# Attention and a mixture of experts on one core: two row groups a slot sooner, and a new list of slots for one batch's token selection

## The chip, the core and the metric

The kernel runs on one core of a Trainium2 chip. The core has a matrix engine (PE, with its weight loads shown apart as PEld), a vector engine (DVE), a scalar engine (ACT), a general engine (POOL) and a queue engine that starts transfers (SP). Each runs its own list of instructions in order; semaphores join them. The metric is the time of one execution in microseconds of the device, the median of several.

## The reference, cut to what matters

Attention with a causal mask, then a top-1 mixture of experts in which each of 8 experts keeps its 80 best tokens by gate weight.

```python
scores = scale * np.matmul(q, k.transpose(0, 1, 3, 2))      # batch 8, heads 12, seq 448, dim 64, float32
scores = np.where(mask, -1000000000.0, scores)
attn = np.exp(scores - np.max(scores, axis=-1, keepdims=True))
attn = attn / (np.sum(attn, axis=-1, keepdims=True) + 1e-09)
x = np.matmul(attn, v)                                      # then (batch * seq, heads * dim) = 3584 x 768
logits = x @ w_gate                                         # 8 experts
expert_idx = np.argmax(logits, axis=1)                      # gate_w: the softmax weight of that expert
for e in range(E):
    tok_idx = np.where(expert_idx == e)[0]
    if len(tok_idx) > capacity:                             # 80
        tok_idx = tok_idx[np.argpartition(-gate_w[tok_idx], capacity)[:capacity]]
    h = np.maximum(x[tok_idx] @ w1[e], 0.0)
    out[tok_idx] = gate_w[tok_idx, None] * (h @ w2[e])
```

## The kernel before, in words

**The work.** Two heads make a pair; there are 6 pairs to a batch and 48 in all (pair 0 to pair 47). Attention runs as a pipeline over pairs. While the loop stands at pair i, PE issues the score products of pair i + 1 (`sp`, at the end of the pair), turns the exponentials of pair i - 1 (`tp`, four groups of four 128x128 transposes) and multiplies those of pair i - 2 by the values (`xp`, 16 matmuls). For pair i itself DVE makes the shifted scores (L444, seven pieces of 192, 192, 320, 320, 448, 448 and 64 columns, with their row minima) and ACT the exponentials (L448, the same seven). ACT copies the first three groups of `tp` to SBUF (L487), DVE the fourth; ACT copies `xp` into the batch's output `xu` (L510).

**The order.** The kernel writes the order out by hand. The loop gives each pair 8 slots, and each engine gets its instructions in the order in which the slots name them:

```python
TSLOT = [0, 1, 2, 4]                      # slots of the four tp groups
COPIED = {1: (0, 1), 2: (2,), 5: (3,)}    # slot: tp groups that are copied
SHIFTED = [0, 0, 1, 2, 3, 4, 4]           # slots of the seven pieces on DVE
VSLOT, XSLOT = 5, 6                       # xp, and its copy
```

In a slot first comes what these tables name (`tp`, `xp`, DVE's pieces, copies of `tp`, one exponential, the copy of `xp`), and then what the dictionary `plan` holds for that slot. `plan` holds what is done once per batch, in slots counted from the batch's end, that is, during the pairs of the next batch and the one after. There are two kinds of it.

- Row groups (`row_group`; `ROWS0` and `ROWS1`). A batch's output stands head by head in `xu`. A row group turns three 128x128 blocks back to token rows (`rt`, L604), DVE multiplies them by the reciprocal sums into `xr` (L623), and SP stores `xr` to `xs` in HBM (L628). A batch has eight; the two numbers of each are the slot of the turn and the slot of DVE's part.
- The selection (`STEPS`, and `EARLY` for the seventh batch, whose next batch is the last): `gp` and `lp` make the gate logits; `r0t` and `r1t` turn one-hot rows and weights (`selt`, L737) and `r0c`, `r1c` copy them to `ex`; `rl`, `lt` and `cp` count against the table of the batches before (`cp`, L780); `places` and `places2` are two DVE instructions that read `cp` into `rm` (L800); `c3w` to `c0w` multiply (`rn`, L751) and `c3l` to `c0l` compare (`less`, L754) inside the batch; `gt`, `own`, `rank`, `rr`, `tn`, `tab`, `rp`, `row` make the new table.

A batch's selection reaches into the pairs of the second batch after it: slot 52 (`cp`) is slot 4 of the pair at which the next batch has just ended. The first batch has no table before it and so no `cp`. So pairs 18, 24, 30, 36 and 42 have both the row groups of one batch and the `cp` of the batch before; pair 6 has row groups alone, and pair 12 row groups and comparisons. Below, these seven are called row pairs.

**The buffers.** All of `tp`, `xp`, `rt`, `cp`, `rn`, `gp`, `lp`, `selt`, `rl`, `gt`, `tn` and `rp` come from one pool of four PSUM buffers (`ps_g`, tag `g`); the score products have four others. A new tile of this pool can be written only when one of the four tiles before it has been read for the last time, and the pool gives it the buffer of one of these at build time.

**After attention** a tail written out by hand (`TAIL`) finishes the last pair and the last batch's selection; a gather (L1209) fetches the first expert's 80 rows, and with it SP starts the remaining weight loads (L222). Then come the two layers of the eight experts.

Of the kernel before, what the change touches and what calls it, by code (L numbers as in the profile page):

```python
# [24 lines left out]
SHIFTED = [0, 0, 1, 2, 3, 4, 4]  # L25
VSLOT, XSLOT = 5, 6
NORMS = [0, 2, 4]
ROWS0 = [(3, 5), (4, 6), (9, 10), (19, 20)]
ROWS1 = [(27, 28), (35, 36), (36, 38), (40, 41)]
STEPS = {'gp': 20, 'gs': 22, 'lp': 24, 'lg': 25, 'logit': 26, 'shifted': 27, 'chosen': 32, 'sums': 33, 'one_hot': 33, 'columns': 33, 'weight': 35, 'weighted': 36, 'parts': 37, 'r0t': 41, 'r0c': 42, 'r1t': 42, 'r1c': 43, 'rl': 44, 'lt': 46, 'c3w': 49, 'c3l': 50, 'cp': 52, 'ro': 53, 'places': 54, 'c2w': 56, 'c2l': 57, 'places2': 57, 'c1w': 58, 'c1l': 59, 'c0w': 59, 'c0l': 60, 'earlier': 60, 'gt': 65, 'own': 67, 'rank': 67, 'rr': 68, 'tn': 73, 'tab': 74, 'rp': 76, 'row': 78}  # L30
EARLY = {'gp': 16, 'gs': 18, 'lp': 24, 'lg': 25, 'logit': 26, 'shifted': 26, 'chosen': 28, 'sums': 29, 'one_hot': 29, 'columns': 29, 'weight': 30, 'weighted': 30, 'parts': 30, 'r0t': 32, 'r0c': 33, 'r1t': 33, 'r1c': 34, 'rl': 34, 'lt': 35, 'c3w': 35, 'c3l': 36, 'c2w': 36, 'c2l': 38, 'cp': 40, 'ro': 40, 'places': 41, 'c1w': 41, 'c1l': 42, 'c0w': 42, 'c0l': 43, 'places2': 43, 'earlier': 43, 'gt': 44, 'own': 45, 'rank': 45, 'rr': 46, 'tn': 49, 'tab': 49, 'rp': 52, 'row': 53}
THIRD = [0, 0, 2, 2, 4, 6, 8]
THIRD_EARLY = [0, 2, 4, 6, 6, 8, 9]
SECOND = [5, 6, 7, 8, 9, 10, 11]
# [13 lines left out]
def attention_then_moe(  # L48
# [907 lines left out]
    def later_on(slot, stages, gap=1):  # L956
        for x, f in enumerate(stages):
            plan.setdefault(slot + x * gap, []).append(f)
        return slot + len(stages) * gap

    def batch_plan(bt):

        ends = (bt.b * NP + NP) * SLOTS
        for x, f in zip(NORMS, norms(bt, slice(0, NP))):
            later_on(ends + x, [f])
        for g, rows in enumerate((ROWS0, ROWS1)):
            for t in range(NT):
# [5 lines left out]
        if CAP:  # L973
            steps.update(select_groups(bt))
        for name, at in (EARLY if bt.b == B - 2 else STEPS).items():
            if name in steps:
# [467 lines left out]
```

## Time and profile before

| | |
|---|---|
| median of 3 runs | 472.04 us (470.94 to 473.41) |
| profiled execution, its own time | 474.3 us |
| its span, first to last instruction | 472.5 us |
| mean granted TensorE clock | 0.987 |
| busy share of the span: PE, PEld, DVE, ACT, POOL | 92%, 70%, 81%, 83%, 51% |

The profiled execution's time is 1.8 us more than its span; its time is 2.3 us over the median of the runs. The busy shares are means over three stages: attention to about 327 us, the tail to about 355 us, and the experts. In a timeline row the first number is the start in us from the span's start, the second the stretch that the row's instructions took, then engine, line, operation, tiles (out<-in), shape, count, and in brackets the idle time of the engine just before and what ended it.

### The profile page before, as it was taken

What the parts mean: (1) busy time and instruction counts of PE and PEld (TensorE: products, weight loads), DVE (VectorE), ACT (ScalarE), POOL (GpSimd) and SP (SyncE); (2) the same over time, 40 slices, a digit from 0 to 9 for tenths busy, and PEclk for the clock granted to TensorE, in tenths of its full rate; (3) what the DMA queues carried; (4) which work ended last, traced back from release to release, by engine and by line L of the source; (5) the groups of instructions that cost most, each with busy time, mean ns of one, the idle gap of its engine ahead of it and who ended that gap; (6) DMA issues with size and microseconds to landing.
All of it is one profiled execution on the core that took longest, in us unless ns stands there. A gap on an engine that the chain in (4) does not pass through costs nothing.

```text
span 472.5 us, 15193 instructions
## 1 busy us (share of the span) xinstructions
PE 434.1 (92%) x5539; PEld 329.2 (70%) x5539; DVE 381.9 (81%) x1313; ACT 393.1 (83%) x1058; POOL 242.5 (51%) x359
## 2 busy tenths in 40 slices
PE   7799999999899899989989998989789999999894
PEld 3566677667567667756766775656549999999894
DVE  6676788978868887886888788696668999999991
ACT  5889999989879888987988898786477999899881
POOL 7957727718455851845575184510354265533511
PEclk9799999999999999999999999999989999999999
DMA  8454848748466563745665374359729999999941
GB/s 258 134 197 156 260 159 296 237 128 287 155 200 219 203 209 102 265 169 179 219 210 201 108 256 173 102 199 389 312 69 300 386 384 385 385 406 409 399 156 43
DMA packets 46666, 109.90 MB, mean 233 GB/s; under 512 B 5842, under 2 KB 23250, under 8 KB 45952
## 3 DMA queue, kind: packets, MB, share of 16 engines
q1 hardware_dynamic: 45392, 105.20, 63.3%
q0 software_dynamic: 1056, 3.51, 2.3%
q8 instruction: 43, 0.70, 0.6%
q14 instruction: 31, 0.25, 0.2%
q10 hardware_dynamic: 144, 0.23, 0.2%
HBM read 85.35 MB, written 23.99 MB: 231 GB/s over the span
## 4 chain that ended last, share of the span: by engine, by line
PE 65%; ACT 16%; issue 6%; DMA 5%; DVE 4%; POOL 3%; POOLq 0%; ACTq 0%; DVEq 0%
PE xp L505 18%; PE sp L425 11%; ACT PT L487 10%; PE tp L482 9%; ACT prob L448 5%; DMA wraw<-w 4%; PE gp L558 3%; PE hp L1242 2%; PE hp L1251 2%; PE hp L1249 2%; PE op L1252 2%; PE hp L1252 2%; PE rt L604 2%; PE op L1251 2%; PE op L1249 2%
## 5 line engine op out<-in xcount | busy, mean ns | idle before, releaser
L448 ACT ACTIVATE prob<-ns,nb 128x192 f32<-128x192 f32 (+3 forms) x336 | 176.0, 531 | 16.6 <-DVE nb L444 15.8
L444 DVE CUSTOM_DVE_ANT_0 ns<-sp,mask 128x192 f32<-128x192 f32 (+3 forms) x336 | 135.1, 445 | 47.2 <-PE sp L425 43.9
L482 PE MATMUL tp<-ident,prob 128*128 128x128 f32 x768 | 112.2, 280 | 4.5 <-ACT PT L487 4.2
L505 PE MATMUL xp<-PT,vt 128*64 128x448 f32 (+3 forms) x768 | 94.8, 389 | 10.4 <-issue 6.9
L373 POOL TENSOR_TENSOR qk<-qk,qk 128x448 f16<-128x448 f32 x94 | 96.7, 1044 | 7.1 <-DVE qk L401 3.9
L1173 DVE SCALAR_TENSOR_TENSOR wl<-wraw,wh 128x768 f16<-128x768 f32 (+1 forms) x98 | 97.3, 1060 | 1.7 <-POOL wl L1364 1.6
L487 ACT COPY PT<-tp 128x512 f32<-128x512 f32 x144 | 81.7, 586 | 15.8 <-PE tp L482 14.8
L505 PEld LDWEIGHTS xp<-PT,vt 128*64 128x64 f32 x768 | 52.3, 137 | 59.2 <-issue 32.8
L482 PEld LDWEIGHTS tp<-ident,prob 128*128 128x128 f32 x768 | 85.9, 143 | 9.0 <-ACT PT L487 6.7
L1188 ACT ACTIVATE wh<-wraw 128x768 f16<-128x768 f32 (+1 forms) x98 | 84.8, 925 | 3.2 <-PE hp L1252 0.9
L425 PE MATMUL sp<-qk 64*128 64x448 f16 (+2 forms) x864 | 68.3, 297 | 3.6 <-POOL qk L373 2.8
L1252 PEld LDWEIGHTS <-wl 128*128 128x128 f16 x668 | 66.7, 100 | 2.8 <-issue 2.7
L1249 PEld LDWEIGHTS <-wh 128*128 128x128 f16 x668 | 67.1, 100 | 1.9 <-issue 1.9
L1251 PEld LDWEIGHTS <-wh 128*128 128x128 f16 x668 | 66.7, 100 | 0.4 <-issue 0.3
L448 ACT ACTIVATION_READ_ACCUMULATOR prob<-ns,nb 128x1 f32 x336 | 65.7, 195 | 0.0
L1330 POOL DMA_INDIRECT out<-yo,idx x8 | 35.6, 4456 | 53.6 <-ACT yo L1327 50.4
L425 PEld LDWEIGHTS <-qk 64*128 64x128 f16 x864 | 36.4, 94 | 18.6 <-issue 2.9
L487 DVE COPY PT<-tp 64x256 f32<-64x256 f32 x144 | 43.6, 328 | 4.1 <-PE tp L482 2.0
L1251 PE MATMUL op<-hl,wh 128*128 128x80 f16 x324 | 36.8, 202 | 1.3 <-issue 1.3
L1249 PE MATMUL hp<-xh,wh 128*128 128x80 f16 x320 | 36.4, 202 | 1.1 <-issue 1.1
L1249 PE MATMUL op<-hh,wh 128*128 128x80 f16 x324 | 36.8, 202 | 0.3 <-issue 0.3
L1251 PE MATMUL hp<-xl,wh 128*128 128x80 f16 x320 | 36.2, 202 | 1.0 <-DVE xl L1228 0.7
(179 smaller groups left out, 659.4 us busy)
## 6 DMA issues: line engine op xcount, KB each, us to landing
wraw<-w SPq DMA_DIRECT2D x48, 384.0 KB
wraw<-w SPq DMA_DIRECT2D x30, 512.0 KB
out<-mask SPq DMA_DIRECT2D x56, 192.0 KB
qk<-k_t SPq DMA_DIRECT2D x23, 448.0 KB
qk<-q_t SPq DMA_DIRECT2D x23, 448.0 KB
vt<-v_t SPq DMA_DIRECT2D x24, 384.0 KB
xs<-xr SPq DMA_DIRECT2D x42, 192.0 KB
wraw<-w SPq DMA_DIRECT2D x5, 1536.0 KB
```

What stands on the lines that cost most here:

```text
L373: sub = lambda e, o, a, b: e.tensor_tensor(out=o, in0=a, in1=b, op=ALU.subtract)
L425: nc.tensor.matmul(pr.sp[t, j], a[rows, p, queries(t)], c[rows, p, FROM[t]:FROM[t] + WIDTH[t]], start=(x == 0), stop=(x == 2))
L444: nc.vector.tensor_tensor_reduce(out=ns, in0=pr.sp[x], in1=m, scale=-1.0 / 8.0, scalar=HUGE, op0=ALU.add, op1=ALU.min, accum_out=nb)
L448: nc.scalar.activation(pr.P[:, OFF[x]:OFF[x] + w], got[0], AF.Exp, bias=got[1], scale=-1.0, accum_out=pr.sums[:, h:h + 1])
L482: nc.tensor.transpose(tp[:, i * P:(i + 1) * P], f, ident)
L487: way(part_of(pr.PT, rows, to, *todims), part_of(got[0], rows, at, *dims))
L505: nc.tensor.matmul(xp[rows, c * P:S], st["vt"][:, c, p * P + j * DH:p * P + (j + 1) * DH], pr.PT[:, j, n0:n0 + w], start=(c == 0), stop=(c ...
L1173: return nc.vector.scalar_tensor_tensor(out=l, in0=src, scalar=SW, in1=h, op0=ALU.mult, op1=ALU.subtract)
L1188: nc.scalar.activation(h, src, AF.Copy, scale=SW)
L1249: nc.tensor.matmul(o, wh[:, ws], ah[:, c, :], start=(x == 0 and i % per == 0), stop=False, skip_group_check=True)
L1251: nc.tensor.matmul(o, wh[:, ws], al[:, c, :], start=False, stop=False, skip_group_check=True)
L1252: nc.tensor.matmul(o, wl[:, ws], ah[:, c, :], start=False, stop=(x == n - 1), skip_group_check=True)
```

## The change

Two row groups of every batch move. The turn of the first goes from slot 3 to slot 2 after the batch's end and DVE's part from 5 to 3; the turn of the second from 4 to 3 and DVE's part from 6 to 4. In `STEPS`, `places2` goes from 57 to 54, beside `places`; `ro` goes from 53 to 52 and issues nothing here, since 80 slots fit one chunk. The seventh batch gets another list.

```diff
-ROWS0 = [(3, 5), (4, 6), (9, 10), (19, 20)]
+ROWS0 = [(2, 3), (3, 4), (9, 10), (19, 20)]
...
-EARLY = {'gp': 16, 'gs': 18, 'lp': 24, 'lg': 25, 'logit': 26, 'shifted': 26, 'chosen': 28, 'sums': 29, 'one_hot': 29, 'columns': 29, 'weight': 30, 'weighted': 30, 'parts': 30, 'r0t': 32, 'r0c': 33, 'r1t': 33, 'r1c': 34, 'rl': 34, 'lt': 35, 'c3w': 35, 'c3l': 36, 'c2w': 36, 'c2l': 38, 'cp': 40, 'ro': 40, 'places': 41, 'c1w': 41, 'c1l': 42, 'c0w': 42, 'c0l': 43, 'places2': 43, 'earlier': 43, 'gt': 44, 'own': 45, 'rank': 45, 'rr': 46, 'tn': 49, 'tab': 49, 'rp': 52, 'row': 53}
+EARLY = {'gp': 18, 'gs': 20, 'lp': 24, 'lg': 25, 'logit': 26, 'shifted': 26, 'chosen': 28, 'sums': 29, 'one_hot': 29, 'columns': 29, 'weight': 30, 'weighted': 30, 'parts': 30, 'r0t': 33, 'r0c': 34, 'r1t': 35, 'r1c': 36, 'rl': 36, 'lt': 38, 'c3w': 40, 'c3l': 41, 'c2w': 41, 'c2l': 42, 'c1w': 42, 'c1l': 43, 'cp': 43, 'ro': 43, 'c0w': 44, 'c0l': 45, 'earlier': 45, 'places': 46, 'places2': 46, 'gt': 46, 'own': 47, 'rank': 47, 'rr': 47, 'tn': 49, 'tab': 49, 'rp': 52, 'row': 53}
```

On PE in pair 18 (and in the same way in 24, 30, 36 and 42), with `tp` the transposes of the pair before, `rt` the row groups, `cp` the rank counts and `xp` the product with the values:

```order
 L751 MATMUL rn<-ex 128x512
 L482 MATMUL tp<-ident,prob_108 128x128 x4
-L604 MATMUL rt<-ident,xu 128x128 x3
+L604 MATMUL rt<-ident,xu 128x128 x6
 L482 MATMUL tp<-ident,prob_108 128x128 x4
 L780 LDWEIGHTS lt
@@ -1032,5 +1030,4 @@
 L780 LDWEIGHTS lt
 L780 MATMUL cp<-oh_699,lt 80x8
-L604 MATMUL rt<-ident,xu 128x128 x3
 L505 MATMUL xp<-PT_113,vt_109 64x448 x2
```

Both row groups now stand before the fourth transposes. The four tiles before `xp` were `rt`, `tp`, `cp`, `rt` and are now `rt`, `rt`, `tp`, `cp`. In the built program `xp` took the buffer of the fourth transposes and waited for DVE's copy of them; now it takes the buffer of the first row group and waits for DVE's first `xr`.

On DVE in the same pair, before (the two 448-column pieces, the 64-column piece, the copies of the fourth transposes into `PT`, the first `xr`, the first `rm`, the second `xr`, the next pair's first piece):

```order
L444 ISA ns,nb<-sp,mask 128x448
L444 ISA nb 128x1
L444 ISA ns,nb<-sp,mask 128x448
L444 ISA nb 128x1
L444 ISA ns,nb<-sp,mask_86 128x64
L444 ISA nb 128x1
L487 COPY PT_114<-tp 64x2x2x64
L487 COPY PT_114<-tp 64x2x64 x2
L623 TENSOR_TENSOR xr<-rt,sums 128x384
L800 SCALAR_TENSOR_TENSOR rm<-cp,pnum,slots_e 80x320
L623 TENSOR_TENSOR xr<-rt,sums 128x384
L444 ISA ns,nb<-sp,mask 128x192
```

and now:

```order
L444 ISA ns,nb<-sp,mask 128x448
L444 ISA nb 128x1
L623 TENSOR_TENSOR xr<-rt,sums 128x384
L444 ISA ns,nb<-sp,mask 128x448
L444 ISA nb 128x1
L444 ISA ns,nb<-sp,mask_86 128x64
L444 ISA nb 128x1
L623 TENSOR_TENSOR xr<-rt,sums 128x384
L487 COPY PT_114<-tp 64x2x2x64
L487 COPY PT_114<-tp 64x2x64 x2
L800 SCALAR_TENSOR_TENSOR rm<-cp,pnum,slots_e 80x320 x2
L444 ISA ns,nb<-sp,mask 128x192
```

The first `xr` moved ahead of the pair's last two pieces, the second ahead of the copies into `PT`, and the second `rm` came up from the next pair. On SP the store of the first `xr` now stands ahead of one part of a weight load (or of one block of zeros for the output) instead of behind it.

On PE in pair 46, the second to last, in the seventh batch's selection, behind the last of the `rl` products:

```order
 L767 LDWEIGHTS ex
 L767 MATMUL rl<-row_1_709,ex 128x80
-L604 MATMUL rt<-ident,xu 128x128 x3
-L751 LDWEIGHTS ex
-L751 MATMUL rn<-ex 128x512
-L482 MATMUL tp<-ident,prob_108 128x128 x4
-L604 MATMUL rt<-ident,xu 128x128 x3
-L751 LDWEIGHTS ex
-L751 MATMUL rn<-ex 128x384
 L505 MATMUL xp<-PT_113,vt_109 64x448 x2
```

The two row groups and the fourth transposes now stand further up in the pair, the second turn of `selt` (from `mv`) after the third transposes instead of the second. The two largest `rn` moved into pair 47, where `xp` now stands behind all four `rn` and `gt` behind `xp`. In pair 44 `gp` moved from behind the first transposes to behind the third.

## Rows read from the trace of the kernel before

**Rows 1.** Busy time of the engines in stretches of the span: PE, PEld, DVE, ACT and POOL busy us (with instruction counts), granted clock, DMA share, GB/s. The first stretch is one batch, the others are the tail and the experts.

```profile
123.50:164.80 41.30, 38.76 (x407) 27.39 (x403) 33.59 (x147) 35.32 (x110) 23.19 (x40) 1.00 0.58 192
...
327.20:355.20 28.00, 23.84 (x190) 14.54 (x188) 17.15 (x60) 16.86 (x35) 11.71 (x16) 0.94 0.57 215
355.20:472.50 117.30, 105.72 (x2294) 103.63 (x2294) 104.86 (x122) 96.61 (x148) 45.58 (x14) 0.99 0.87 327
```

**Rows 2.** What PE's matmuls waited for: total us, times, longest.

```profile
PE xp L505 <- issue: 6.9, 5, 1.4
PE tp L482 <- ACT PT L487: 4.2, 8, 0.7
```

**Rows 3.** Timeline of PE in pair 18, from the first row group to `xp`.

```profile
118.59 0.49 PE L604 MATMUL rt<-ident,xu 128*128 128x128 f32 x3
...
119.35 0.28 PE L780 MATMUL cp<-oh,lt 128*80 128x8 bf16 x4
119.75 0.55 PE L604 MATMUL rt<-ident,xu 128*128 128x128 f32 x3
121.67 1.95 PE L505 MATMUL xp<-PT,vt 128*64 128x448 f32 x16 [1.38 <-issue]
```

**Rows 4.** Timeline of DVE over the same time, up to the first piece of pair 19.

```profile
119.03 0.41 DVE L537 RECIPROCAL sums<-sums 128x42 f32<-128x42 f32 x1
119.36 0.56 DVE L444 CUSTOM_DVE_ANT_0 ns<-sp,mask 128x448 f32<-128x448 f32 x1
...
119.84 0.62 DVE L444 CUSTOM_DVE_ANT_0 ns<-sp,mask 128x448 f32<-128x448 f32 x1
...
120.39 0.22 DVE L444 CUSTOM_DVE_ANT_0 ns<-sp,mask 128x64 f32<-128x64 f32 x1
...
120.65 0.92 DVE L487 COPY PT<-tp 64x256 f32<-64x256 f32 x3
121.49 0.54 DVE L623 TENSOR_TENSOR xr<-rt,sums 128x384 f32<-128x384 f32 x1
121.96 0.53 DVE L800 SCALAR_TENSOR_TENSOR rm<-cp,pnum,slots_e 80x320 bf16<-80x320 f32 x1
122.42 0.54 DVE L623 TENSOR_TENSOR xr<-rt,sums 128x384 f32<-128x384 f32 x1
124.53 0.36 DVE L444 CUSTOM_DVE_ANT_0 ns<-sp,mask 128x192 f32<-128x192 f32 x1 [1.57 <-PE sp L425]
```

**Rows 5.** Timeline of ACT over the same time: the copy of the third transposes, the exponential of the second 448-column piece, the copy of `xp`, and the first exponential of pair 19.

```profile
119.11 0.58 ACT L487 COPY PT<-tp 128x512 f32<-128x512 f32 x1
...
121.33 0.67 ACT L448 ACTIVATE prob<-ns,nb 128x448 f32<-128x448 f32 x1
...
123.66 0.53 ACT L510 COPY xu<-xp 128x448 f32<-128x448 f32 x1 [1.24 <-PE xp L505]
124.93 0.46 ACT L448 ACTIVATE prob<-ns,nb 128x192 f32<-128x192 f32 x1 [0.74 <-DVE nb L444]
```

**Rows 6.** Timeline of pair 19, the pair after: DVE's second `rm` and third `xr`, ACT's copy of the third transposes, and PE's fourth transposes.

```profile
126.36 0.54 DVE L800 SCALAR_TENSOR_TENSOR rm<-cp,pnum,slots_e 80x320 bf16<-80x320 f32 x1
...
127.22 0.55 DVE L623 TENSOR_TENSOR xr<-rt,sums 128x384 f32<-128x384 f32 x1
...
127.37 0.59 ACT L487 COPY PT<-tp 128x512 f32<-128x512 f32 x1
...
128.01 0.66 PE L482 MATMUL tp<-ident,prob 128*128 128x128 f32 x4 [0.57 <-ACT PT L487]
```

**Rows 7.** Timeline of pair 6, the first row pair: DVE's first 448-column piece and PE's `xp`.

```profile
42.41 0.56 DVE L444 CUSTOM_DVE_ANT_0 ns<-sp,mask 128x448 f32<-128x448 f32 x1
...
44.39 1.95 PE L505 MATMUL xp<-PT,vt 128*64 128x448 f32 x16 [0.37 <-ACT PT L487]
```

**Rows 8.** Timeline of the seventh batch's selection: the fourth transposes of pair 44; the second `selt`, DVE's two largest comparisons, an `rn` and `xp` of pair 46; the scores, the fourth transposes and `xp` of pair 47; and the first transposes of the tail.

```profile
301.37 0.66 PE L482 MATMUL tp<-ident,prob 128*128 128x128 f32 x4 [0.37 <-ACT PT L487]
...
313.78 0.40 PE L737 MATMUL selt<-identb,mv 128*128 128x128 bf16 x4 [0.84 <-POOL mv L722]
...
317.14 0.73 DVE L754 SCALAR_TENSOR_TENSOR less<-rn,ggw,before 128x512 bf16<-128x512 f32 x1
...
317.26 0.32 PE L751 MATMUL rn<-ex 128*128 128x384 bf16 x1 [0.61 <-DVE xr L623]
317.93 1.95 PE L505 MATMUL xp<-PT,vt 128*64 128x448 f32 x16 [0.35 <-DVE less L754]
...
319.22 0.60 DVE L754 SCALAR_TENSOR_TENSOR less<-rn,ggw,before 128x384 bf16<-128x384 f32 x1
...
319.81 1.40 PE L425 MATMUL sp<-qk 64*128 64x192 f16 x18
...
324.47 0.65 PE L482 MATMUL tp<-ident,prob 128*128 128x128 f32 x4 [0.71 <-ACT PT L487]
...
325.29 1.95 PE L505 MATMUL xp<-PT,vt 128*64 128x448 f32 x16
327.17 0.66 PE L482 MATMUL tp<-ident,prob 128*128 128x128 f32 x4
```

**Rows 9.** Timeline at the end of the tail: the gather of the first expert's rows on POOL, and SP's remaining weight loads.

```profile
350.56 1.08 POOL L1209 DMA_INDIRECT xg<-xs,idx  x1 [4.68 <-DVE gws L934]
...
355.32 16.15 SPq L222 DMA_DIRECT2D wraw<-w  x15
```

More of the change, by code (lines that the diff above doesn't have):

```diff
@@ L27 @@
 NORMS = [0, 2, 4]
-ROWS0 = [(3, 5), (4, 6), (9, 10), (19, 20)]
+ROWS0 = [(2, 3), (3, 4), (9, 10), (19, 20)]
 ROWS1 = [(27, 28), (35, 36), (36, 38), (40, 41)]
-STEPS = {'gp': 20, 'gs': 22, 'lp': 24, 'lg': 25, 'logit': 26, 'shifted': 27, 'chosen': 32, 'sums': 33, 'one_hot': 33, 'columns': 33, 'weight': 35, 'weighted': 36, 'parts': 37, 'r0t': 41, 'r0c': 42, 'r1t': 42, 'r1c': 43, 'rl': 44, 'lt': 46, 'c3w': 49, 'c3l': 50, 'cp': 52, 'ro': 53, 'places': 54, 'c2w': 56, 'c2l': 57, 'places2': 57, 'c1w': 58, 'c1l': 59, 'c0w': 59, 'c0l': 60, 'earlier': 60, 'gt': 65, 'own': 67, 'rank': 67, 'rr': 68, 'tn': 73, 'tab': 74, 'rp': 76, 'row': 78}
-EARLY = {'gp': 16, 'gs': 18, 'lp': 24, 'lg': 25, 'logit': 26, 'shifted': 26, 'chosen': 28, 'sums': 29, 'one_hot': 29, 'columns': 29, 'weight': 30, 'weighted': 30, 'parts': 30, 'r0t': 32, 'r0c': 33, 'r1t': 33, 'r1c': 34, 'rl': 34, 'lt': 35, 'c3w': 35, 'c3l': 36, 'c2w': 36, 'c2l': 38, 'cp': 40, 'ro': 40, 'places': 41, 'c1w': 41, 'c1l': 42, 'c0w': 42, 'c0l': 43, 'places2': 43, 'earlier': 43, 'gt': 44, 'own': 45, 'rank': 45, 'rr': 46, 'tn': 49, 'tab': 49, 'rp': 52, 'row': 53}
+STEPS = {'gp': 20, 'gs': 22, 'lp': 24, 'lg': 25, 'logit': 26, 'shifted': 27, 'chosen': 32, 'sums': 33, 'one_hot': 33, 'columns': 33, 'weight': 35, 'weighted': 36, 'parts': 37, 'r0t': 41, 'r0c': 42, 'r1t': 42, 'r1c': 43, 'rl': 44, 'lt': 46, 'c3w': 49, 'c3l': 50, 'cp': 52, 'ro': 52, 'places': 54, 'c2w': 56, 'c2l': 57, 'places2': 54, 'c1w': 58, 'c1l': 59, 'c0w': 59, 'c0l': 60, 'earlier': 60, 'gt': 65, 'own': 67, 'rank': 67, 'rr': 68, 'tn': 73, 'tab': 74, 'rp': 76, 'row': 78}
+EARLY = {'gp': 18, 'gs': 20, 'lp': 24, 'lg': 25, 'logit': 26, 'shifted': 26, 'chosen': 28, 'sums': 29, 'one_hot': 29, 'columns': 29, 'weight': 30, 'weighted': 30, 'parts': 30, 'r0t': 33, 'r0c': 34, 'r1t': 35, 'r1c': 36, 'rl': 36, 'lt': 38, 'c3w': 40, 'c3l': 41, 'c2w': 41, 'c2l': 42, 'c1w': 42, 'c1l': 43, 'cp': 43, 'ro': 43, 'c0w': 44, 'c0l': 45, 'earlier': 45, 'places': 46, 'places2': 46, 'gt': 46, 'own': 47, 'rank': 47, 'rr': 47, 'tn': 49, 'tab': 49, 'rp': 52, 'row': 53}
 THIRD = [0, 0, 2, 2, 4, 6, 8]
```

## The prediction

> **What bounds the kernel now.** I read the stretches first. In a batch of attention PE is busy 38.76 of 41.30 us, ACT 35.32, DVE 33.59, POOL 23.19, and the transfers take 0.58 of the DMA engines [rows 1]. So PE paces attention, and what can be won there without less work is its idle 2.5 us per batch. Where that lies, PE's waits tell: `xp` waited 6.9 us, five times, 1.4 at the longest, with no engine named ("issue"), and `tp` 4.2 us, eight times, for ACT's copies [rows 2]. Five times 1.4 is 6.9: it is one wait that repeats, and the timeline puts it into pair 18, where `xp` starts at 121.67 after 1.38 us idle [rows 3]. The rows of DVE say why: its copy of the fourth transposes starts at 120.65 and the next instruction at 121.49; `xp` starts as soon as it has ended (120.65 + 0.92 = 121.57) and well before the first `xr` ends (122.03) [rows 4]. So `xp` waits for a buffer, that of the fourth transposes, which DVE empties only behind three pieces of the softmax. The data that `xp` multiplies are a pair old. In pair 19 the fourth transposes start at 128.01 after 0.57 idle; ACT's copy of the third ends at 127.37 + 0.59 = 127.96: again a buffer [rows 6].
>
> The end moves with attention's end. The first gather stands at 350.56 and the remaining weight loads start behind it at 355.32 [rows 9]; from there the transfers take 0.87 of the DMA engines, in the tail before only 0.57 [rows 1]. The loads have no head start that a shorter attention could use up, so I let every us won in attention count once in the end.
>
> **The row pairs with `cp` (18, 24, 30, 36, 42).** Nothing is added or removed: the same transposes, multiplications and stores stand elsewhere. `xp` now takes the buffer of the first row group. When is that free? DVE's first 448-column piece ends at 119.36 + 0.48 (starts 119.36 and 119.84), by then the reciprocals (119.03 + 0.41) and the turn (118.59 + 0.49) are done, so `xr` runs from 119.84 to 120.38 with the 0.54 of its own row [rows 3, 4]. The 0.07 from 121.57 to PE's start, taken over with the matmul's 0.03 behind its weights, gives `xp` at 120.48 instead of 121.67: 1.19 us. PE itself would be ready at about 120.0: `cp`, last before `xp` now, waits for ACT's copy of the third transposes (119.11 + 0.58 = 119.69), as the second row group does now at 119.75, and takes 0.28 [rows 3, 5]. So a wait of some 0.3 to 0.4 stays.
>
> What pays for it is the two `xr` ahead of softmax pieces. The second 448-column piece ends 0.47 later, at 120.39 + 0.47 = 120.86; ACT takes it up at 121.33 [rows 4, 5], so the delay is covered with 0.4 to spare. Were that cover gone, the exponentials and then the copies that free buffers would be late by what is missing. Behind it DVE runs without a gap: from 119.84 two `xr` (0.47 each from start to start), the pieces (0.55 and 0.26), the copies (0.84) and two `rm` (0.46 each) make 3.5 us, to 123.35 [rows 4]. The next pair's first piece starts at 124.53, on scores that come 1.19 sooner now, at 123.34 [rows 4]. So DVE is just in time. It loses its 1.57 us of idle, and ACT its 1.24 and some of its 0.74 [rows 5]. Each 0.1 by which I have DVE too fast costs 0.1 per batch.
>
> **The pair after (19, 25, 31, 37, 43).** The second `rm`, at 126.36, is gone from here, 0.46 of DVE's time, so the third `xr` ends at 127.22 + 0.55 - 0.46 = 127.31. The fourth transposes take its buffer and start at 127.37 instead of 128.01; `xp` behind them takes the third transposes' buffer, free at 127.96 as before, where it used to follow the fourth transposes (128.01 + 0.66, less some 0.07 that matmuls overlap) [rows 6]. It starts at about 128.04 instead of 128.6: 0.55 us.
>
> Both together are 1.74 us for each of five batches, 8.7 us. Bounds: 1.19 alone (ACT or DVE keep the second), 5.95; all idle of both rows, 5 x (1.38 + 0.57) = 9.75.
>
> **Pairs 6 and 12.** Pair 6 has no `cp`. There `xp` waits 0.37 for ACT's copy of the third transposes [rows 7]; now it takes the first row group's buffer, whose `xr` can end at 42.41 + 0.56 + 0.54 = 43.51, before PE is there. 0.3 us, between 0 and 0.37. In pair 12 the buffers of `xp` and of the transposes before it stay those of the same copies: nothing.
>
> **The seventh batch's list.** In pair 44 `gp` comes behind the third transposes, so the fourth no longer wait 0.37 for ACT's copy of these [rows 8]: 0.4 us with the pipeline's drain. In pair 46 PE waits 0.84 for POOL's `mv`, 0.61 for an `xr` and 0.35 for a comparison, and `xp` starts at 317.93 [rows 8]. Now the fill before `mv` is a group of transposes and a row group more, the two `rn` are gone, and `xp` waits for DVE's copy of the second `selt`: `mv` at 313.78 as now, two pieces, an `xr` and the copy behind it, about 316.1. So pair 46 is 1.8 us shorter. Pair 47 takes over the two `rn` and DVE's two comparisons (0.73 and 0.60), and `xp` there waits for the third comparison behind them: 5.85 us after the pair's scores by DVE's durations, where it is 325.29 - 319.81 = 5.48 now; `gt` follows `xp` and waits for the last comparison. The tail's first transposes come 8.3 us after the scores instead of 327.17 - 319.81 = 7.36 [rows 8]. So 0.9 of the 1.8 is given back. The list is worth 0.4 + 0.9 = 1.3 us; bounds are all its waits, 0.37 + 0.84 + 0.61 + 0.35 + 0.71 = 2.9, and, since the last pair's chain through DVE is long and I add it up by hand, a loss of 1.5 (its 0.9 more, and the 0.6 of one comparison that PE would stand behind in the tail).
>
> **The queues.** SP now stands at the first store until its `xr` is done, with one weight part or zero block behind it. Those parts are multiplied only after 355 [rows 9], so this is free. POOL's order does not change.
>
> **Sum.** 8.7 + 0.3 + 1.3 = 10.3 us. The profiled execution's 474.3 would be 464.0, its span 472.5 would be 462.2; the median of the runs, 2.3 lower than the profiled time, goes from 472.04 to 461.7.
>
> **The rivals.**
> *Half of it.* The bubble at `xp` shrinks, and the rest is eaten by DVE, which has no slack left, or by the last pairs. 5.95 alone gives 466.1. For it: DVE's 0.01 us of margin. Against: DVE has less to do in the pair after.
> *All of it.* PE never waits in these places: 9.75 + 0.37 + 2.9 gives 459.0. Against: the first `xr` ends at 120.38 by the rows, and PE is ready earlier.
> *The idle moves and nothing is won.* ACT is busy 35.32 of 41.30 us, 86%, PE's weight loads only 27.39, 66% [rows 1]; if ACT paces the batch, PE's bubble is only where the surplus shows, and each bubble closed opens another. Then only the seventh list counts: 470.7. Against: ACT itself idles 1.24 for `xp` behind the bubble and 0.74 more [rows 5], and 6 us per batch in all. The Trainium skill, Perfetto Trace Analysis, section Identifying the Most-Contended Engine, says this: matmul busy time is no measure of the tensor engine's headroom, weight-load busy time is, and for the other engines occupancy tells the one to work on. By that rule ACT is the engine here, and the time stays near 471. The trace's waits of ACT for PE speak against it in these pairs.
> *Slower.* DVE is late with the first `xr`: 1.2 us later than I have it and `xp` starts no sooner than now; if it came only behind DVE's copies, at 122.41 (121.57 + the 0.94 of two `xr` - 0.1 of gaps now there), each of the five batches would lose 0.74, 3.7 us, and with the list's loss of 1.5 the time would be 477.2, without it 475.7. It decides itself at whether `xr` ends before 121.57. Against: all that it needs is there by 119.84.
>
> **How the numbers follow.** The forecast (459.5 to 464.5) gets 0.62, half of it (464.5 to 468.5) 0.20, all of it 0.08, nothing won 0.06, slower 0.04. The range 458.5 to 467.5 takes in the bounds of the first three and leaves out some 0.15. Half a percent, about what a measurement of this kernel can tell from no change, is 2.4 us: faster 0.90, same 0.06, slower 0.04.
>
> **What would show it.** In the trace after: `xp` of pair 18 with 0.2 to 0.5 us idle instead of 1.38, released by the first `xr`; a batch of 39.5 us instead of 41.2; the fourth transposes of pair 19 with no wait for ACT; DVE without the 1.57 us before pair 19's first piece; pair 46 near 7.8 us and pair 47's first tail transposes about 8.3 us after its scores. The prediction is wrong if DVE's first piece of pair 19 comes late after its scores, if ACT's copies become what `tp` and `xp` wait for elsewhere in the batch, or if the tail or the experts grow by what attention loses.

## The result and the profile after

The changed kernel takes 460.12 us (median of 4 runs, 459.66 to 461.18); the kernel before took 471.58 beside it (470.94 to 473.41). The ratio is 0.9754, with a 95% interval from 0.9721 to 0.9787: 11.5 us faster. The forecast was 461.7. The profiled execution took 460.32 us, its span 458.5, at a mean granted clock of 0.990.

A batch of attention (the same stretch as the first of [rows 1], from pair 19's scores to pair 25's), with the columns of [rows 1]:

```profile
120.19:159.58 39.39, 38.35 (x405) 27.25 (x402) 33.52 (x148) 35.17 (x111) 23.11 (x40) 1.00 0.60 200
```

It is 1.9 us shorter, and every engine's busy time is what it was to about 0.4 us: it is mostly idle time that went. PE idles 1.0 us per batch instead of 2.5. Its waits, which answer to [rows 2]:

```profile
PE xp L505 <- DVE xr L623: 2.1, 5, 0.4
PE tp L482 <- DVE xr L623: 1.3, 6, 0.2
PE tp L482 <- ACT PT L487: 0.5, 1, 0.5
```

The five waits of 1.4 us with no engine named are gone; five of 0.4 for `xr` stand in their place. Of `tp`'s eight waits for ACT one is left. The timeline of PE through pairs 18 and 19 shows both:

```profile
116.45 0.82 PE L604 MATMUL rt<-ident,xu 128*128 128x128 f32 x6
117.11 0.60 PE L482 MATMUL tp<-ident,prob 128*128 128x128 f32 x4
117.61 0.28 PE L780 MATMUL cp<-oh,lt 128*80 128x8 bf16 x4
...
118.31 1.95 PE L505 MATMUL xp<-PT,vt 128*64 128x448 f32 x16 [0.42 <-DVE xr L623]
...
124.02 0.66 PE L482 MATMUL tp<-ident,prob 128*128 128x128 f32 x4 [0.22 <-DVE xr L623]
124.61 1.95 PE L505 MATMUL xp<-PT,vt 128*64 128x448 f32 x16
```

DVE over the same time, from the first 448-column piece to the first piece of pair 19 (as [rows 4]), and ACT's first exponential of pair 19:

```profile
117.22 0.56 DVE L444 CUSTOM_DVE_ANT_0 ns<-sp,mask 128x448 f32<-128x448 f32 x1
117.70 0.55 DVE L623 TENSOR_TENSOR xr<-rt,sums 128x384 f32<-128x384 f32 x1
118.17 0.61 DVE L444 CUSTOM_DVE_ANT_0 ns<-sp,mask 128x448 f32<-128x448 f32 x1
118.71 0.22 DVE L444 CUSTOM_DVE_ANT_0 ns<-sp,mask 128x64 f32<-128x64 f32 x1
118.86 0.55 DVE L623 TENSOR_TENSOR xr<-rt,sums 128x384 f32<-128x384 f32 x1
119.44 0.92 DVE L487 COPY PT<-tp 64x256 f32<-64x256 f32 x3
120.29 0.99 DVE L800 SCALAR_TENSOR_TENSOR rm<-cp,pnum,slots_e 80x320 bf16<-80x320 f32 x2
121.21 0.34 DVE L444 CUSTOM_DVE_ANT_0 ns<-sp,mask 128x192 f32<-128x192 f32 x1
```
```profile
121.59 0.46 ACT L448 ACTIVATE prob<-ns,nb 128x192 f32<-128x192 f32 x1 [0.74 <-DVE nb L444]
```

The first `xr` ends at 118.25 and `xp` starts at 118.31. The 1.57 us that DVE idled before pair 19's first piece are gone; ACT's 0.74 for that piece is as in [rows 5], so DVE came just in time.

The seventh batch's selection: scores and `xp` of pair 46, scores, fourth transposes, `xp` and `gt` of pair 47, and the tail's first transposes (compare [rows 8]):

```profile
297.98 1.40 PE L425 MATMUL sp<-qk 64*128 64x192 f16 x18
...
303.43 1.95 PE L505 MATMUL xp<-PT,vt 128*64 128x448 f32 x16
305.31 1.40 PE L425 MATMUL sp<-qk 64*128 64x192 f16 x18
...
310.00 0.66 PE L482 MATMUL tp<-ident,prob 128*128 128x128 f32 x4 [0.53 <-ACT PT L487]
...
310.90 1.95 PE L505 MATMUL xp<-PT,vt 128*64 128x448 f32 x16 [0.19 <-DVE less L754]
312.81 0.41 PE L817 MATMUL gt<-oh,less 128*128 128x8 bf16 x10
313.08 0.63 PE L482 MATMUL tp<-ident,prob 128*128 128x128 f32 x4
```

**The account.** I measured every pair in both traces from its first scores to those of the next pair:

| place | before | after | won |
|---|---|---|---|
| pairs 18, 24, 30, 36, 42, each | 7.95 | 6.73 | 1.22 (6.1 together) |
| pairs 19, 25, 31, 37, 43, each | 6.92 | 6.29 | 0.63 (3.15 together) |
| pair 6 | 6.87 | 6.54 | 0.33 |
| pair 44 | 8.40 | 7.58 | 0.82 |
| pair 46 | 9.60 | 7.33 | 2.27 |
| pair 47, to the tail's first transposes | 7.36 | 7.77 | -0.41 |
| pair 5 | 5.18 | 5.34 | -0.16 |
| ahead of pair 3 | 23.85 | 21.92 | 1.93 |

That is 14.0 us, which is all the difference of the two spans. The last two rows are not the change's. For the last the experiments show it below; pair 5 takes anything from 5.18 to 5.48 us in the traces, and in the two of the changed kernel itself 5.34 and 5.48. Without these rows 12.3 us are left, and the medians differ by 11.5.

### The profile page after: what moved, and what is told of

Same layout as the page of the kernel before. It is cut to its first block, busy times and chain, and to the rows that moved or that the text cites. A ratio compares the mean times of both kernels' runs of the same rounds, so it can differ in the third digit from the quotient of the medians.

```text
span 458.5 us, 15186 instructions
## 1 busy us (share of the span) xinstructions
PE 430.1 (94%) x5539; PEld 327.5 (71%) x5539; DVE 381.2 (83%) x1313; ACT 392.3 (86%) x1058; POOL 240.1 (52%) x359
## 5 line engine op out<-in xcount | busy, mean ns | idle before, releaser
L482 PE MATMUL tp<-ident,prob 128*128 128x128 f32 x768 | 110.9, 278 | 1.8 <-DVE xr L623 1.3
L505 PE MATMUL xp<-PT,vt 128*64 128x448 f32 (+3 forms) x768 | 93.6, 386 | 5.2 <-DVE xr L623 2.1
L505 PEld LDWEIGHTS xp<-PT,vt 128*64 128x64 f32 x768 | 51.0, 136 | 52.5 <-issue 23.6
L1330 POOL DMA_INDIRECT out<-yo,idx x8 | 34.1, 4260 | 55.5 <-ACT yo L1327 52.4
L425 PEld LDWEIGHTS <-qk 64*128 64x128 f16 x864 | 36.4, 94 | 18.6 <-issue 2.9
L1252 PE MATMUL hp<-xh,wl 128*128 128x80 f16 x320 | 36.2, 202 | 2.1 <-issue 2.0
L1252 PE MATMUL op<-hh,wl 128*128 128x80 f16 x324 | 36.9, 202 | 0.4 <-issue 0.3
```

The costliest lines, as they stand in the source:

```text
L425: nc.tensor.matmul(pr.sp[t, j], a[rows, p, queries(t)], c[rows, p, FROM[t]:FROM[t] + WIDTH[t]], start=(x == 0), stop=(x == 2))
L482: nc.tensor.transpose(tp[:, i * P:(i + 1) * P], f, ident)
L505: nc.tensor.matmul(xp[rows, c * P:S], st["vt"][:, c, p * P + j * DH:p * P + (j + 1) * DH], pr.PT[:, j, n0:n0 + w], start=(c == 0), stop=(c ...
L1252: nc.tensor.matmul(o, wl[:, ws], ah[:, c, :], start=False, stop=(x == n - 1), skip_group_check=True)
```

## The experiments

The theory: `xp` waits for its PSUM buffer; DVE emptied it late, and the new order gives it one that is emptied sooner. The pair after is a second matter (the second `rm` ahead of the third `xr`), the seventh list a third. All kernels compute the whole result. "Pair 18" stands for the five pairs with `cp` and "pair 19" for the five after them; they agree within 0.01 us in every trace unless said.

### One part of the change at a time: e1, e2, e3

e1 has the new row slots alone, e2 the new `STEPS` alone, e3 the new `EARLY` alone (of the long lists only what changes is shown; `ro`, which issues nothing, moves in e2 as well):

```diff
e1: -ROWS0 = [(3, 5), (4, 6), (9, 10), (19, 20)]
e1: +ROWS0 = [(2, 3), (3, 4), (9, 10), (19, 20)]
e2: -'places2': 57
e2: +'places2': 54
e3: the new EARLY of the change
```

> The kernel before with the new slots of the two row groups alone; second rm and the seventh batch's list as before. Buffer theory: xp of pair 18 takes the first row group's buffer and waits for its xr, as in the changed kernel, so its idle falls from 1.38 to about 0.4 us in each of the five pairs with cp (1.2 us each, 6.1 together) and pair 6 gives 0.3; pair 19 keeps its wait of about 0.5 us at the fourth transposes, because the second rm still stands ahead of the third xr there and DVE is not quicker: about 6.4 us in all, near 465. Rival (both edits are needed, DVE would stall at rm): idle at xp stays over 1 us, 470 or more. Rival (the second rm is free anyway): 9.6 us in all, near 462, with no wait in pair 19.

> The kernel before with only the second rm moved beside the first (slot 54). Theory of buffers: xp of pair 18 still takes the fourth transposes' buffer and keeps its 1.38 us idle; the second rm now ahead of the second xr costs nothing for PE there; in pair 19 the third xr ends 0.46 us sooner and the wait of 0.57 us of the fourth transposes shrinks: 0 to 3 us in all, near 470. Rival (DVE's load behind xp delays the next pair): pair 19's first piece comes late and the time is 471 to 473.

> The kernel before with only the seventh batch's new list. By my sum of before's rows 1.3 us, near 470.3; by the trace of the changed kernel 2.7 us (pair 44 0.8, pair 46 2.3, pair 47 gives 0.4 back), near 468.9. Pairs 18 to 43 keep their 1.38 and 0.57 us waits.

| kernel | median us | ratio to before (471.41) | pair 18 | pair 19 | pairs 44, 46 |
|---|---|---|---|---|---|
| e1 | 465.51 | 0.9861 (0.9825 to 0.9896) | 6.73 | 6.92 | 8.40, 9.59 |
| e2 | 468.56 | 0.9944 (0.9913 to 0.9974) | 7.95 | 6.29 | 8.40, 9.60 |
| e3 | 469.37 | 0.9945 (0.9923 to 0.9967) | 7.95 | 6.92 | 7.58, 7.33 |

Each part moves its own pairs, by what the whole change moves there (e1 pair 6 too), and from pair 3 on no other by more than the 0.3 us by which a single pair can differ between executions: 5.9, 2.9 and 2.0 us by the medians, 10.8 together. PE in e1 has the short wait at `xp`, and in pair 19 still the old one of [rows 6]; in e2 it is the other way round:

```profile
118.13 1.95 PE L505 MATMUL xp<-PT,vt 128*64 128x448 f32 x16 [0.43 <-DVE xr L623]
...
124.46 0.66 PE L482 MATMUL tp<-ident,prob 128*128 128x128 f32 x4 [0.57 <-ACT PT L487]
```
```profile
119.63 1.95 PE L505 MATMUL xp<-PT,vt 128*64 128x448 f32 x16 [1.38 <-issue]
...
125.33 0.66 PE L482 MATMUL tp<-ident,prob 128*128 128x128 f32 x4 [0.23 <-DVE xr L623]
```

So the row slots made the 1.22 and the second `rm` the 0.63, and neither needs the other. Both rivals of e1 fall, and that of e2.

### What `xp` waits for: e4, e5, e6

Three placements of the two row groups, each on the kernel before:

```diff
-ROWS0 = [(3, 5), (4, 6), (9, 10), (19, 20)]
e4: +ROWS0 = [(2, 5), (3, 6), (9, 10), (19, 20)]
e5: +ROWS0 = [(3, 4), (4, 6), (9, 10), (19, 20)]
e6: +ROWS0 = [(3, 5), (6, 7), (9, 10), (19, 20)]
```

> The kernel before with the two turns a slot sooner on PE but DVE's parts where they were (slots 5 and 6). Buffer theory: xp is released by what DVE does last before it: its buffer (by the build that of the copies of the fourth transposes, which stand ahead of both xr on DVE) is free at the old time, so xp keeps about 1.4 us idle, and the time stays within 1 us of before, 470.5 to 472.5. Rival (the order on PE alone makes the gain, since the second turn no longer stands between cp and xp): idle at xp near 0.4 us and about 6 us gained, near 465.5.

> The kernel before with the first row group's DVE part one slot sooner (slot 4), the turns where they were. Buffer theory: by the build xp takes the first row group's buffer here, and its xr now stands ahead of the copies of the fourth transposes but behind all the pair's softmax pieces; from before's rows it ends near 121.15 us (120.61 and 0.54), 0.4 us ahead of the old release, so xp's idle is 0.9 to 1.0 us instead of 1.38 and the kernel gains about 0.4 five times: 2.1 us, near 469.3. Rival (what counts is that the second turn is gone from between cp and xp): no gain, 471.4. Rival (any xr ahead of the copies gives the whole gain): 6 us.

> The kernel before with the second row group turned behind xp (slots 6 and 7) and the first as before: no xr comes sooner. Buffer theory: by the build xp of the pairs with cp then takes the third transposes' buffer, which ACT empties at 119.69 us of before's timeline; so xp's idle all but goes (below 0.3 us) without any xr ahead of a softmax piece; 1.2 us or more five times, though the second turn now stands behind xp and moves its 0.4 us, so nothing is lost by it: 5 to 7 us, near 465.5. Rival (xp waits for data that DVE makes, or for DVE's load as such): idle at xp stays 1.4 us, 471.4.

| kernel | median us | ratio to before | pair 18 |
|---|---|---|---|
| e4 | 471.32 | 0.9981 (0.9961 to 1.0000) | 7.95 |
| e5 | 468.93 | 0.9947 (0.9928 to 0.9967) | 7.42 |
| e6 | 464.87 | 0.9878 (0.9852 to 0.9904) | 6.56 |

(The median of before was 471.41 beside e4 and 471.12 beside e5 and e6.) PE and then DVE of e4 in pair 18:

```profile
117.96 0.28 PE L780 MATMUL cp<-oh,lt 128*80 128x8 bf16 x4
119.88 1.95 PE L505 MATMUL xp<-PT,vt 128*64 128x448 f32 x16 [1.64 <-issue]
```
```profile
118.86 0.92 DVE L487 COPY PT<-tp 64x256 f32<-64x256 f32 x3
```

PE has the order of the changed kernel up to `xp`, and nothing is won: without the row group between `cp` and `xp` the wait grows from 1.38 to 1.64. `xp` starts 0.10 behind the end of DVE's copies (118.86 + 0.92 = 119.78), as it did before (121.57 and 121.67). The release is DVE's, whatever PE does ahead of it.

In e5 only the first `xr` moves ahead of those copies. `xp` follows its end (118.54 + 0.55 = 119.09); the gain lies between nothing and that of the whole change, as it must if the time of the release decides: 0.53 per pair, a little over the 0.4 expected:

```profile
119.15 1.95 PE L505 MATMUL xp<-PT,vt 128*64 128x448 f32 x16 [0.85 <-DVE xr L623]
```
```profile
118.54 0.55 DVE L623 TENSOR_TENSOR xr<-rt,sums 128x384 f32<-128x384 f32 x1
```

e6 moves no `xr` forward; it only shifts a turn behind `xp`, so that `xp` takes the buffer of the third transposes, which ACT empties:

```profile
115.96 0.28 PE L780 MATMUL cp<-oh,lt 128*80 128x8 bf16 x4
116.35 1.95 PE L505 MATMUL xp<-PT,vt 128*64 128x448 f32 x16
```
```profile
115.72 0.58 ACT L487 COPY PT<-tp 128x512 f32<-128x512 f32 x1
```
```profile
117.25 0.92 DVE L487 COPY PT<-tp 64x256 f32<-64x256 f32 x3
```

`xp` starts 0.05 behind the end of ACT's copy (116.30), no wait is listed any more, and pair 18 is shorter than in the changed kernel. DVE's work and its order ahead of `xp` are those of before, and its copies of the fourth transposes, behind which `xp` stood in before and in e4, start only 0.90 behind `xp` here (the last row). That leaves no room for the rival that `xp` waits for DVE's data or load: it waited for a buffer. The Trainium skill names this cause (Perfetto Trace Analysis, Optimization Strategy): the same gap, repeated on the engine that should be full, can mean that there is no room in PSUM for the next tile. This trace agrees, with 1.38 us five times and none once the buffer is another.

### The seventh list, one step of it: e7

```diff
-EARLY = {'gp': 16, 'gs': 18, ...
+EARLY = {'gp': 18, 'gs': 20, ...
```

> The kernel before with gp and gs of the seventh batch two slots later and the rest of its list as before; it touches pair 44 alone. By my sum 0.4 us (471.0), by the trace of the changed kernel 0.8 us (470.6): pair 44 from scores to scores 8.0 or 7.6 us instead of 8.4.

Measured: 471.76 us, ratio 1.0015 (0.9992 to 1.0037). The runs do not show a gain of 0.8 us; taken as it stands, the interval ends at a gain of 0.4. In the trace pair 44 takes 7.58 us instead of 8.40 and every later pair what it took before. So the 0.82 of the account comes from `gp` alone; as a time of the kernel it stays unresolved. The recorded clocks can account for the contradiction, without proving it. The mean granted clock of e7's ten runs was 0.992, that of before beside it 0.996. Of e7's own runs the two at 0.997 took 469.2 and 469.8 us, the five at 0.989 took 471.5 to 472.7: about 0.3 us for each 0.001, so that 0.004 would hide some 1.2 us (an estimate from these runs). A median of a few runs can mislead by about 1 us here.

### What is left in the changed kernel: e8 to e11, and the changed kernel again

The changed kernel still waits 0.42 at `xp` and 0.22 at the next pair's fourth transposes. Four kernels move the first `xr` (e9), the third (e10), both (e8), and both with the second `rm` behind pair 19's first two pieces (e11):

```diff
-ROWS0 = [(2, 3), (3, 4), (9, 10), (19, 20)]
e8, e11: +ROWS0 = [(2, 2), (3, 4), (9, 9), (19, 20)]
e9:      +ROWS0 = [(2, 2), (3, 4), (9, 10), (19, 20)]
e10:     +ROWS0 = [(2, 3), (3, 4), (9, 9), (19, 20)]
e11: -'places2': 54
e11: +'places2': 56
```

> The changed kernel with the first xr one slot sooner (slot 2, ahead of the first 448-column piece) and the third xr one slot sooner (slot 9). In the changed kernel xp of the pairs with cp still waits 0.42 us for the first xr, and the fourth transposes of the next pair 0.22 us for the third xr. If buffers alone count: both waits go, 5 x 0.42 + 6 x 0.22 = 3.4 us, near 456.7. If DVE has no slack left there, the softmax pieces come later by 0.47 us, ACT's exponentials and copies follow, and the next pair's transposes wait instead: 459 to 461, no gain.

> The changed kernel itself once more, beside the next three on the same chip. Attention from pair 2 on as before (pair 18 6.73, pair 19 6.29 us from scores to scores); time near 460. If the 2 us by which the profiled executions differ ahead of pair 2 come from the granted clock of that execution and not from the kernel, the length of pairs 0 and 1 can be another here, between 15 and 19 us, with the kernel unchanged; if they belong to the kernel, it is 16.7 us again.

> The changed kernel with only the first xr one slot sooner. If each wait is worth its own length: pair 18 is 0.3 shorter, pair 19 as it is (6.29), 1.5 us in all, near 458.6. If DVE has no slack left between the two: the third xr comes later by what pair 18 gained, the fourth transposes of pair 19 wait 0.4 to 0.5 us instead of 0.22, pair 19 is 6.5 to 6.6, and 0 to 0.5 us are gained, near 459.8.

> The changed kernel with only the third xr one slot sooner. Its wait of 0.22 us at the fourth transposes goes. If that wait is worth its own length: 6 x 0.22 = 1.3 us, near 458.8. If ACT's copy of the third transposes, which ends 0.2 us before xp in the changed kernel (124.45 against 124.61), takes over: xp of pair 19 comes 0.05 to 0.1 sooner, 0.3 to 0.6 us in all, near 459.7.

> The changed kernel with the first and the third xr a slot sooner and the second rm behind the next pair's two first pieces (slot 56), with PE's order that of e8. There DVE reached pair 19's first piece late and ACT idled 1.08 us for it; now it is reached 0.46 sooner. If that lateness is what held pair 19 at 6.30 us: 6.1 to 6.2, 0.5 to 1 us less than e8, near 456.6. If the copies of the transposes hold it whatever DVE does: 6.30, and 457.4.

| kernel | median us | ratio to before | pair 18 | pair 19 |
|---|---|---|---|---|
| changed, again | 459.86 | 0.9738 (0.9712 to 0.9764) | 6.73 | 6.29 |
| e9 | 459.41 | 0.9730 (0.9701 to 0.9758) | 6.42 | 6.54 |
| e10 | 458.42 | 0.9703 (0.9677 to 0.9729) | 6.73 | 6.19 |
| e8 | 457.38 | 0.9709 (0.9686 to 0.9732) | 6.42 | 6.30 |
| e11 | 456.43 | 0.9676 (0.9649 to 0.9703) | 6.42 | 6.19 |

(Before: 471.12 beside e8, which ran ahead of the others, and 472.06 beside these; so e8 is compared by its pairs.) In e9 pair 18 gives 0.31 and pair 19 takes 0.25 of it back: the second of its two expectations, but for the wait. DVE has no gap left between the two pairs, so the third `xr` comes all but as late as it did. The wait listed for it at the fourth transposes is still 0.23 and not the 0.4 to 0.5 expected; most of the 0.25 is lost further up, since the third transposes already start 3.01 us after the pair's scores instead of 2.83 (PE of pair 19):

```profile
123.08 0.66 PE L482 MATMUL tp<-ident,prob 128*128 128x128 f32 x4 [0.23 <-DVE xr L623]
```

In e10 the wait for the third `xr` goes, but pair 19 gains 0.10, not 0.22: `xp` starts at 124.28, right behind ACT's copy of the third transposes, which ends at 123.65 + 0.57 = 124.22:

```profile
124.28 1.95 PE L505 MATMUL xp<-PT,vt 128*64 128x448 f32 x16
```
```profile
123.65 0.57 ACT L487 COPY PT<-tp 128x512 f32<-128x512 f32 x1
```

By the pairs e10 is worth 0.6 us; its median, 1.4 us under the changed kernel's, is nearer to the other expectation, but the intervals overlap, its runs had the higher mean clock (0.996 against 0.992), and I go by the pairs. e8 has both moves, and neither of its expectations holds: both waits are gone from the list, pair 18 keeps its gain of 0.31, but pair 19 stays at 6.30: ACT's first exponential of pair 19 is late because DVE is. In e11 one `rm` less stands ahead of that piece. ACT of e8 and of e11:

```profile
121.86 0.46 ACT L448 ACTIVATE prob<-ns,nb 128x192 f32<-128x192 f32 x1 [1.08 <-DVE nb L444]
```
```profile
121.46 0.46 ACT L448 ACTIVATE prob<-ns,nb 128x192 f32<-128x192 f32 x1 [0.62 <-DVE nb L444]
```

ACT waits 0.46 less, one `rm`, and pair 19 falls to 6.19. e11 beats both kernels: its interval ends below that of the changed kernel run beside it. The pairs account for 2.2 of the 3.4 us between the two medians.

**The 1.9 us ahead of pair 3.** This stretch holds pairs 0, 1 and 2; where the expectation of the changed kernel's second run says "pairs 0 and 1" and "from pair 2 on", pairs 0 to 2 and pair 3 are meant. The changed kernel, run again, has 15.25 us in these three pairs together, where its first profile had 16.70 and the kernel before 18.59. Stretches from 15 us on, with the columns of [rows 1] (the granted clock is the third number from the end), of the kernel before, of the changed kernel, and of it again:

```profile
15.00:18.00 3.00, 2.13 (x21) 1.55 (x21) 2.00 (x10) 1.79 (x8) 2.81 (x5) 0.72 0.01 3
18.00:21.00 3.00, 3.00 (x16) 2.67 (x16) 1.83 (x9) 2.34 (x6) 2.58 (x7) 0.50 0.49 134
21.00:24.00 3.00, 3.00 (x20) 1.42 (x22) 0.86 (x3) 2.50 (x11) 3.00 (x4) 0.64 0.83 243
```
```profile
15.00:18.00 3.00, 2.65 (x21) 1.69 (x21) 2.06 (x10) 1.73 (x8) 2.81 (x5) 0.63 0.01 3
18.00:21.00 3.00, 3.00 (x20) 2.35 (x20) 2.56 (x10) 2.41 (x6) 2.58 (x7) 0.80 0.50 138
```
```profile
15.00:18.00 3.00, 2.34 (x28) 1.77 (x23) 2.41 (x10) 2.75 (x12) 2.81 (x4) 1.00 0.03 8
18.00:21.00 3.00, 3.00 (x33) 1.97 (x33) 2.27 (x10) 3.00 (x11) 2.58 (x8) 1.00 0.61 184
```

The same kernel has the drop of the clock in one execution and not in another, so it is the execution's and not the change's.

## Why the prediction was right, point by point

**What bounds the kernel.** PE's idle time at two places per batch: right. They gave 1.22 + 0.63 = 1.85 of the 2.5 us that PE idled in a batch.

**Pairs with `cp`, 1.19 each:** 1.22. The remaining wait of 0.3 to 0.4, released by the first `xr`: 0.42, for that `xr`. e4 and e6 show the mechanism. The listed wait fell by 0.96 only. The other 0.26 lies ahead of it: from the first row group to the end of what stands before `xp` PE took 1.71 us (118.59 to 119.75 + 0.55 [rows 3]) and takes 1.44 now (116.45 to 117.61 + 0.28), since the second group no longer stands alone behind `cp`. My sum went from start to start of `xp` and so had both. In e4 the same 0.26 goes into a longer wait.

**The pair after, 0.55 each:** 0.63, and e2 has it by itself. That the fourth transposes would then follow the third `xr`: so they do, after 0.22 us of idle PE. They start 3.83 us after the pair's scores (124.02 - 120.19), and the sum had 3.82 (127.37, with the scores at 123.55). What it had too late is `xp` behind them: I left ACT's copy of the third transposes where it was, 4.41 us after the scores, and it ended after 4.26.

**DVE just in time:** right at pair 19's first piece, which starts 1.02 us after the pair's scores (121.21 - 120.19) where it was 0.98 in before. e9 shows how exactly: where pair 18 gives DVE 0.31 us less time, 0.25 comes back in pair 19.

**Pair 6, 0.3; pair 12, nothing:** 0.33, and 6.05 both times.

**The seventh list, 1.3: mis-sized.** It is 0.82 + 2.27 - 0.41 = 2.7 in the trace; e3's median says 2.0 (1.6 to 3.6 by its interval). Three terms of that step were mis-sized, each to the small side of the gain. In pair 44 I counted the listed wait of 0.37 and not the stops too short for the list. In pair 46 I started DVE's two pieces with the second `selt`, at 313.78, although they don't need it; by the trace after the first of them starts before POOL has the `mv` (301.23 + 0.25 = 301.48), and the copy that frees `xp`'s buffer comes sooner (the 448-column piece, the copy, then POOL's last `mv`):

```profile
301.27 0.60 DVE L444 CUSTOM_DVE_ANT_0 ns<-sp,mask 128x448 f32<-128x448 f32 x1
...
302.97 0.40 DVE L740 COPY ex<-selt 24x512 bf16<-24x512 bf16 x1
```
```profile
301.23 0.25 POOL L722 TENSOR_TENSOR mv<-grest,mv 128x32 bf16<-128x32 f32 x1
```

`xp` comes 5.45 us after the pair's scores; I had 5.9. In pair 47 I had `xp` 5.85 after the scores and `gt` waiting for the last comparison behind it, 8.3 in all. `xp` came after 5.59, and `gt` did not wait: it starts at 312.81, as `xp` ends. This reading is of the trace alone: of the list's steps only `gp` was tried by itself.

**Every us of attention counts once:** from the tail's first transposes to the gather 23.4 us in both traces, from there to the end 122.0 in both. So the stores that SP now waits for cost nothing there.

**The sum.** By the pairs it should have been 12.3 where I had 10.3, and 1.4 of the difference is the seventh list, the rest the 0.03 and 0.08 in each of the ten pairs. By the medians side by side the change is worth 11.5; that they stand nearer to my sum than the pairs do is luck.

**The rivals.** *Half of it* (466.1) fell: DVE was in time to 0.04 us. *All of it* (459.0) came near in time, but not by its mechanism: waits of 0.42 and 0.22 stayed, and what made up for them are stops that no wait listed, such as the 0.26 ahead of `xp`. *The idle moves* (470.7) fell: ACT, busy 86% of the batch before, has all but the same 35.2 us in a batch of 39.39, 89%, and e11's batch of 38.97 is shorter still. By the rule of the Trainium skill's Perfetto Trace Analysis (Identifying the Most-Contended Engine), which goes by occupancy and for the tensor engine by weight loads and MFU (the share of its peak rate, not worked out here), ACT was the engine to work on. The measurement decides otherwise: PE's waits showed the way here and the shares did not. *Slower* fell: the first `xr` ended where the rows put it.

## What to carry to other kernels

When a wait repeats at one instruction and the profile names no engine, look at which engine's work ends just before each start, and ask which buffer that work empties: the pool here gives the next tile the buffer of one of the four before it, and which one follows at build time from the order of the tiles and of those who read them, so moving a tile (e6) or a reader (e5) changes who is waited for. Taking waits away on the pacing engine pays only until the engine that empties the buffers has no gap left; from there moves give in one pair what they take in the next, and what pays is to take that engine's work out from ahead of what the others need. Start a chain by hand from what each instruction needs, not from where its neighbour stands.

## What the runs showed of the hardware

I had not expected the clock at the start to differ between executions of one kernel. The granted clock falls to 0.50 (1.2 of 2.4 GHz) for some us between about 15 and 24 us in some executions and stays at 1.00 in others; pairs 0 to 2 together took from 15.2 us (e6, e7) to 18.6 (the kernel before), and the profiled execution of before, on which the prediction's sum was made, had the longest such stretch of all that were profiled. Ahead of it, from 10 to 15 us, PE was busy 3.00 us in before, 2.94 in the changed kernel, 3.44 in the changed kernel's second profile, which had no drop, 2.96 in e9's, which had none in these stretches either, and 3.44 in e10's, which had one. What decides it these runs don't tell. Comparing pair by pair, instead of span by span, keeps it out.
